# Attention scores on 32 rows per head, with zero matmuls in place of repeated score matmuls

## The chip, the cores and the metric

The kernel runs on one core of a Trainium2 chip. The metric is device time of one launch in microseconds (us), median over the runs. Engines are called by their names in the profile: PE multiplies matrices, PEld loads its stationary operand, ACT applies functions element by element, DVE does vector work, POOL a few small things and some of the transfers, SP issues most transfers.

## What is computed

Two layers, each an attention block A and a token-mixing block B, both with a residual. Sequence S = 2048, width D = 640, 32 heads of 20 columns, F = 1536, inputs in bf16.

```python
def _A_ref(x, wqkv, wo):
    qkv = (x @ wqkv).reshape(B, S, 3, H, Dh) ...
    q, k, v = qkv[0], qkv[1], qkv[2]
    scores = jnp.einsum("bhqd,bhkd->bhqk", q, k) * (Dh ** -0.5)
    p = _softmax(scores, axis=-1)
    o = jnp.einsum("bhqk,bhkd->bhqd", p, v)
    return o ... @ wo

def _B_ref(x, w1, b1, w2, b2):
    h = _layernorm(x, axis=-1)
    u = gelu(jnp.einsum("bsd,sf->bdf", h, w1) + b1)
    return (jnp.einsum("bdf,fs->bds", u, w2) + b2) transposed

x = x + _A_ref(_layernorm(x), A_wqkv, A_wo)
x = x + _B_ref(_layernorm(x), ...)
x = x + _A_ref(_layernorm(x), A_wqkv, A_wo)
x = x + _B_ref(_layernorm(x), ...)
```

Each layer has 32 x 2048 x 2048 scores, 134 million, and every one goes through an exponential on ACT.

## The kernel before

**Stages.** A first stage normalizes x and forms the values V and the first head group's keys and queries. Then follow, for each layer, `attention`, `mixer_mm1` and `mixer_mm2`; the mixer of layer 0 also prepares the attention of layer 1. The change lies in `attention`, which runs twice.

**Layout.** Heads go in 8 groups of 4. A group's transposed keys `KT` and queries `QTq` have 128 partitions: each head's 20 rows stand at the start of a block of 32, and the other 12 rows are zero. `Vaug` holds 20 value columns, a column of ones (which yields the softmax denominator) and padding to 32 columns for each head.

**Units and tiles.** A unit is one block of 512 queries (`qb`, 4 of them), one head group `g` (8) and one block of 128 keys (`kt`, 16), 512 units in all. A unit has four chunks, one per head, each of 128 keys x 512 queries. `HORDER` gives the heads' order in a unit. Three chunks in a row, across unit borders, make one PSUM tile `S` of 128 x 1536; there are 683 a layer (the last has two chunks). `S` has two buffers (6 PSUM banks), the output accumulator `acc` one bank, the tile `misc` for all other products one bank.

**Scores** (`s_matmul`, L320). The stationary operand is `KT` on 64 rows, that is two heads' keys at once. So that only one head's score comes out, the moving operand is a copy of the queries in which every second head's rows are multiplied by zero: `prep_block` makes `qev` and `qod` on DVE (L279, L280), once for each of the 32 pairs of query block and group in a layer. Heads 0 and 2, or 1 and 3, lie on different halves of the rows, and `HORDER` (0, 2, 1, 3) puts such a pair side by side.

**The repeat** (`emit_S`). If no other product is planned for the tile, the tile's three score matmuls are issued twice (`R_DEFAULT=1`); the second pass writes the same values again, and the exponential waits for the last of them.

**Exponential** (`emit_exp`, L348): one ACT instruction a tile, 128 x 1536 from PSUM to a bf16 tile `P` (5 buffers).

**Outputs** (`emit_PV`, L546): four matmuls a unit, each with 128 rows and 32 columns of `Vaug`, into the four 32-partition quarters of `acc`. After the last key block `normalize` reads `acc` on DVE (L357 to L364), and the next group takes the one `acc` buffer.

**Order.** PE executes in the order the program is written, held by a chain over all its instructions. For each tile t the loop emits the scores of tile t+1, the exponential of t, the outputs whose exponentials are complete up to tile t-1 (none or one unit), and then some fills. Fills are the other products of the stage: key and query projections (L227), the output projection (L448, L481), the first part of the token-mixing product (L421). `emit_fills` takes 1.5 units of cost if the tile has outputs and 3 if not, and pauses one tile after each finished group; `planned_fill` says beforehand whether there will be any.

The scores of tile t+1 wait for the exponential of t-1, because it reads the same `S` buffer. The scheduling loop:

```python
for t in range(NTILES):
    has_fill = planned_fill()
    reps = 0 if has_fill else CFG["R_DEFAULT"]
    if t + 1 < NTILES:
        emit_S(t + 1, reps)
    emit_exp(t)
    ...
    emit_fills(CFG["FILL_PV"] if n_pv else CFG["FILL_NOPV"], misc_alloc)
```

Of the kernel before, what the change touches and what calls it, by code (L numbers as in the profile page):

```python
# [11 lines left out]
BF16 = mybir.dt.bfloat16  # L12
F32 = mybir.dt.float32
ACT = mybir.ActivationFunctionType
ALU = mybir.AluOpType
# [9 lines left out]
VW = 24  # L25

CFG = dict(
    R_DEFAULT=1,
    FILL_NOPV=3.0,
    FILL_PV=1.5,  # L30
    PV_LAGT=1,
# [8 lines left out]
def kernel(  # L40
# [12 lines left out]
    nc = tc.nc  # L53
# [4 lines left out]
    NKT = NT  # L58
# [6 lines left out]
    def pe(inst):  # L65
        tc.chain_iter_dep("pe_order", inst.ins)
        return inst
# [12 lines left out]
    consts = ctx.enter_context(tc.tile_pool(name="consts", bufs=1))  # L80
# [6 lines left out]

    ident = consts.tile([128, 128], BF16, name="ident")
    make_identity(nc, ident[:])
    mask_ev = consts.tile([128, 1], F32, name="mask_ev")  # L90
    mask_od = consts.tile([128, 1], F32, name="mask_od")
    for blk in range(4):
        nc.vector.memset(mask_ev[32 * blk:32 * blk + 32, :], 1.0 if blk % 2 == 0 else 0.0)
        nc.vector.memset(mask_od[32 * blk:32 * blk + 32, :], 0.0 if blk % 2 == 0 else 1.0)
    mhalf = consts.tile([128, 1], F32, name="mhalf")
    nc.vector.memset(mhalf[:], -0.5)
    warm = consts.tile([128, 1], F32, name="warm")
    nc.gpsimd.tensor_tensor(out=warm[:], in0=mhalf[:], in1=mhalf[:], op=ALU.mult)
    nc.gpsimd.tensor_tensor(out=warm[:], in0=warm[:], in1=mhalf[:], op=ALU.pow)
    x1lp = ctx.enter_context(tc.tile_pool(name="x1lp", bufs=1))  # L100
    x1last = x1lp.tile([128, 4, D], F32, name="x1last")
    hhp = ctx.enter_context(tc.tile_pool(name="hhp", bufs=1))
# [92 lines left out]
    def get_QT(st, qb):  # L195
        if qb not in st.QTq:
            st.QTq[qb] = st.qtp.tile([128, NG, 512], BF16, name="QTq")
        return st.QTq[qb]
# [45 lines left out]
    def attention(st, x_in_ap, x_mid, uacc_l):  # L244
        layer = st.layer
        KT, hT = st.KT, st.hT
        with ExitStack() as p1:
# [7 lines left out]
            ustg = p1.enter_context(tc.tile_pool(name=f"ustg{layer}", bufs=2))  # L255
            h2_tiles = {}
            ptp = p1.enter_context(tc.tile_pool(name=f"ptp{layer}", bufs=CFG["PT_BUFS"]))
            qmp = p1.enter_context(tc.tile_pool(name=f"qmp{layer}", bufs=2))
            atp = p1.enter_context(tc.tile_pool(name=f"atp{layer}", bufs=2))
            x1acc = {}  # L260
            LASTQB = NQB - 1
# [1 line left out]

            units = [(qb, g, kt) for qb in range(NQB) for g in range(NG) for kt in range(NKT)]
            NU = len(units)
            S_tiles, P_tiles, acc_tiles, qm_tiles, attnT_tiles = {}, {}, {}, {}, {}
            fill_queue = deque()
            fill_state = dict(cur=None, idx=0, tile=None, cooldown=0, unit=0)
            proj_enqueue_done = [False]
            in_attention = [True]  # L270
            tt_state = {}

            def prep_block(qb, g):
                if (qb, g) in qm_tiles:
                    return
                qe = qmp.tile([128, 512], BF16, name="qev")
                qo = qmp.tile([128, 512], BF16, name="qod")
                src = get_QT(st, qb)[:, g, :]
                nc.vector.tensor_scalar(out=qe[:], in0=src, scalar1=mask_ev[:, 0:1], scalar2=None, op0=ALU.mult)  # L279
                nc.vector.tensor_scalar(out=qo[:], in0=src, scalar1=mask_od[:, 0:1], scalar2=None, op0=ALU.mult)  # L280
                qm_tiles[(qb, g)] = (qe, qo)

            HORDER = (0, 2, 1, 3)
            chunks = [(n, j) for n in range(NU) for j in HORDER]
            NCH = len(chunks)
            NTILES = (NCH + 2) // 3

            def on_unit_start(n):
                qb_n, g_n, kt_n = units[n]
                fill_state["unit"] = n  # L290
                if qb_n == 0 and kt_n == 0:
                    if g_n + KQA < NG:
                        enqueue_kq_for_group(g_n + KQA)
                    if g_n == max(0, NG - KQA) and NQB > 1:
                        enqueue_qproj(1)
                if qb_n >= 1 and g_n == 0 and kt_n == 2 and qb_n + 1 < NQB:
                    enqueue_qproj(qb_n + 1)
                if not proj_enqueue_done[0]:
                    last_k_block = max(0, NG - 1 - KQA)
                    if NQB == 1:  # L300
                        done = (qb_n == 0 and g_n >= last_k_block)
                    elif NQB == 2:
                        done = (qb_n == 0 and g_n >= max(0, NG - KQA)) or qb_n >= 1
                    else:
                        done = (qb_n == NQB - 2 and (g_n > 0 or kt_n >= 2)) or qb_n > NQB - 2
                    proj_enqueue_done[0] = done
                check_hT_dead()
                if kt_n == 0:
                    ensure_ready(qb_n, g_n)
                    prep_block(qb_n, g_n)  # L310
                if kt_n == NKT // 2 and n + NKT < NU:
                    nqb, ng, _ = units[n + NKT - kt_n]
                    if ("Q", nqb, ng) not in pending_keys():
                        prep_block(nqb, ng)

            def s_matmul(St, slot, n, j):
                qb, g, kt = units[n]
                jj = j // 2
                q = qm_tiles[(qb, g)][j % 2]
                pe(nc.tensor.matmul(St[:, slot, :], lhsT=KT[64 * jj:64 * jj + 64, g, kt * 128:(kt + 1) * 128],  # L320
                                    rhs=q[64 * jj:64 * jj + 64, :], start=True, stop=True,
                                    tile_position=(64 * jj, 0)))

            def emit_S(t, reps):
                cs = chunks[3 * t:3 * t + 3]
                for (n, j) in cs:
                    if j == HORDER[0]:
                        on_unit_start(n)
                St = sps.tile([128, 3, 512], F32, name="S")
                S_tiles[t] = St  # L330
                for _rep in range(reps + 1):
                    i = 0
                    while i < len(cs):
                        n, j = cs[i]
                        if i + 1 < len(cs) and cs[i + 1][0] == n and (j, cs[i + 1][1]) in ((0, 2), (1, 3)):
                            s_matmul(St, i, n, j)
                            s_matmul(St, i + 1, n, cs[i + 1][1])
                            i += 2
                        else:
                            s_matmul(St, i, n, j)  # L340
                            i += 1

            def emit_exp(t):
                St = S_tiles.pop(t)
# [176 lines left out]
            def pending_keys():  # L521
                keys = set()
                if fill_state["cur"] is not None:
                    keys.add(fill_state["cur"]["key"])
                for grp in fill_queue:
                    keys.add(grp["key"])
                return keys
# [9 lines left out]
            def emit_PV(n):  # L537
# [23 lines left out]
            def emit_fills(budget, pool_alloc):  # L561
                fs = fill_state
                if fs["cooldown"] > 0:
                    fs["cooldown"] -= 1
                    return 0.0
                spent = 0.0
                while spent < budget:
                    if fs["cur"] is None:
                        if not fill_queue:
                            break  # L570
                        if fill_queue[0].get("not_before", 0) > fs["unit"] and budget < 100:
                            break
# [12 lines left out]
                return spent  # L585
# [10 lines left out]

            LAGT = CFG["PV_LAGT"]
            pv_done = 0
            emit_S(0, 0)
            for t in range(NTILES):  # L600
                has_fill = planned_fill()
                reps = 0 if has_fill else CFG["R_DEFAULT"]
                if t + 1 < NTILES:
                    emit_S(t + 1, reps)
                emit_exp(t)
                n_pv = 0
                while pv_done < NU and (4 * pv_done + 3) // 3 <= t - LAGT:
                    emit_PV(pv_done)
                    pv_done += 1
                    n_pv += 1  # L610
                emit_fills(CFG["FILL_PV"] if n_pv else CFG["FILL_NOPV"], misc_alloc)
            in_attention[0] = False
            while pv_done < NU:
# [245 lines left out]
```

## Time and profile before

| | |
|---|---|
| time, median of 3 runs | 2105.06 us (2104.55 to 2106.12) |
| the profiled execution: time, span | 2106.7 us, 2104.9 us |
| exponentials of layer 0, first start to last end | 49.79 to 972.49 us |
| exponentials of layer 1, first start to last end | 1093.53 to 2017.59 us |
| PE matmuls in the span | 13278 |
| of them scores (L320), outputs (L546) | 6014, 4096 |
| mean granted clock of PE | 0.992 |

The span runs from the first to the last instruction. "Busy" of PE counts a matmul up to its modelled end, 0.376 to 0.39 us for 512 columns, while the next one of the same kind starts 0.2155 us later; so a PE that is busy all the time need not be full. The granted clock is 1.00 or 0.50 in any one moment. It was 0.50 from the start to 18.2 us (as far as the records reach), from 973.9 to 991.0, from 1086.6 to 1090.0, from 2021.8 to 2035.5 us and at the very end, and 1.00 in all other places. Its changes all lie on one grid of 3.413 us.

### The profile page before, as it was taken

Reading aid. Unit: us, or ns where it says so; the run is one execution under the profiler, and the core shown is the slowest. Engines: PE = TensorE matmul, PEld = TensorE weight load, DVE = VectorE, ACT = ScalarE, POOL = GpSimd, SP = SyncE. Lnnn points to the kernel's source line nnn. Section 1 sums busy time; section 2 is a strip of 40 time slices with the busy share of each in tenths; the row PEclk is TensorE's granted clock in tenths of the full one; section 3 lists DMA queues with packets and bytes.
Section 4 is the critical chain, followed back from the end, with each engine's and each line's share of the span. In section 5 each row is a group of like instructions: output and inputs, shape, how many; then the busy total and the mean of one; then the engine's idle time right before and its main releaser. Section 6 shows DMA issues by size and latency. Waiting matters only on the chain.

```text
span 2104.9 us, 31825 instructions
## 1 busy us (share of the span) xinstructions
PE 1953.5 (93%) x13278; PEld 657.3 (31%) x13278; DVE 570.0 (27%) x1231; ACT 1931.5 (92%) x1504; POOL 148.2 (7%) x218
## 2 busy tenths in 40 slices
PE   7999999999999999997999999999999999999979
PEld 4222222233223332223542222222332233222335
DVE  6122222221322132223642122322113220322242
ACT  5999999999999999996349999999999999999952
POOL 2000000110012001110000000001100120011000
PEclk9999999999999999998999999999999999999989
DMA  5000000110034012223620000001101340222245
GB/s 129 1 1 1 1 18 22 61 53 10 29 58 71 1 35 44 37 26 118 211 81 1 1 1 1 26 28 65 47 14 38 66 63 1 57 49 36 38 121 182
DMA packets 90737, 96.88 MB, mean 46 GB/s; under 512 B 9696, under 2 KB 68192, under 8 KB 90592
## 3 DMA queue, kind: packets, MB, share of 16 engines
q1 hardware_dynamic: 70464, 71.22, 11.0%
q0 software_dynamic: 20128, 23.62, 7.5%
q8 instruction: 104, 1.70, 0.3%
q14 instruction: 41, 0.34, 0.1%
HBM read 55.48 MB, written 39.32 MB: 45 GB/s over the span
## 4 chain that ended last, share of the span: by engine, by line
ACT 58%; PE 25%; issue 13%; DVE 3%; DMA 1%; POOL 0%; SPq 0%; DVEq 0%; ACTq 0%; POOLq 0%
ACT P L348 58%; PE S L320 10%; PE y L741 4%; PE acc L546 3%; PE misc L227 3%; PE pp L218 2%; PE big L670 1%; PE misc L448 1%; DMA ua<-uacc 1%; PE pp L227 0%; DVE T L357 0%; PE S L481 0%; DMA x0in<-in_A_x_dram 0%; DVE bnst L158 0%; PE misc L481 0%
## 5 line engine op out<-in xcount | busy, mean ns | idle before, releaser
L348 ACT ACTIVATE P<-S 128x1536 bf16<-128x1536 f32 (+1 forms) x1366 | 1839.9, 1500 | 8.3 <-PE S L320 7.0
L320 PE MATMUL S<-qev,KT 64*128 64x512 bf16 x2962 | 836.8, 377 | 96.2 <-ACT P L348 90.1
L320 PE MATMUL S<-qod,KT 64*128 64x512 bf16 x3052 | 838.2, 379 | 9.1 <-ACT P L348 4.6
L320 PEld LDWEIGHTS <-KT 64*128 64x128 bf16 x6014 | 326.7, 93 | 655.5 <-issue 486.4
L546 PE MATMUL acc<-P,Vaug 128*32 128x512 bf16 x4096 | 409.9, 389 | 6.2 <-DVE T L357 4.3
L546 PEld LDWEIGHTS <-Vaug 128*32 128x32 bf16 x4096 | 106.5, 92 | 439.0 <-issue 439.0
L427 DVE COPY ustg<-misc 128x512 f32<-128x512 f32 (+1 forms) x144 | 70.0, 486 | 296.6 <-PE misc L421 296.5
L169 POOL TENSOR_TENSOR rstd<-veps,mhalf 128x1 f32<-128x1 f32 x64 | 35.5, 554 | 1187.6 <-DVE veps L164 1068.4
L432 POOL DMA_DIRECT2D uacc<-ustg x96 | 83.0, 864 | 473.6 <-DVE ustg L427 444.3
L421 PE MATMUL misc<-h2st,w1st 128*128 128x512 bf16 (+1 forms) x576 | 115.8, 303 | 0.0
L741 PE MATMUL y<-uT,w2s 128*128 128x512 bf16 (+1 forms) x768 | 107.8, 299 | 3.4 <-ACT uT L684 3.4
L508 DVE CAST QTq<-misc 128x512 bf16<-128x512 f32 x62 | 42.8, 691 | 214.2 <-PE misc L227 214.2
L227 PE MATMUL misc<-hh,wq_pad 128*128 128x512 bf16 x310 | 98.9, 385 | 0.0
L357 DVE STREAM_TRANSPOSE T<-acc 128x512 f32<-128x512 f32 x64 | 45.9, 717 | 186.4 <-PE acc L546 186.4
L508 DVE CAST KT<-misc 128x512 bf16<-128x512 f32 x56 | 38.7, 691 | 212.9 <-PE misc L227 212.9
L227 PE MATMUL misc<-hh,wk_pad 128*128 128x512 bf16 x280 | 87.2, 385 | 0.0
L279 DVE TENSOR_SCALAR qev<-QTq,mask_ev 128x512 bf16<-128x512 bf16 x64 | 22.6, 353 | 235.4 <-PE S L320 234.8
L448 PE MATMUL misc<-wo_pad,attnT 128*128 128x512 bf16 (+1 forms) x384 | 76.8, 303 | 0.0
L741 PEld LDWEIGHTS <-w2s 128*128 128x128 bf16 x768 | 59.6, 98 | 49.9 <-issue 5.0
L76 ACT CAST Vaug<-pp 128x500 bf16<-128x500 f32 (+1 forms) x32 | 14.3, 453 | 52.5 <-PE pp L218 52.5
L457 DVE TENSOR_TENSOR x1s<-misc,xin 128x512 f32<-128x512 f32 (+1 forms) x48 | 23.5, 489 | 131.5 <-PE misc L448 131.5
L218 PE MATMUL pp<-wv,hh 128*128 128x500 bf16 (+1 forms) x320 | 52.0, 313 | 1.7 <-DVE hh L78 1.5
(77 smaller groups left out, 715.9 us busy)
## 6 DMA issues: line engine op xcount, KB each, us to landing
uacc<-ustg POOLq DMA_DIRECT2D x72, 256.0 KB, 4.0
w2s<-in_B_w_dram SPq DMA_DIRECT2D x16, 768.0 KB
w1st<-in_B_w_dram SPq DMA_DIRECT2D x36, 256.0 KB
xd<-x1s SPq DMA_DIRECT2D x24, 320.0 KB
x1in<-xd SPq DMA_DIRECT2D x24, 320.0 KB
ua<-uacc SPq DMA_DIRECT2D x24, 320.0 KB
xd<-x2s SPq DMA_DIRECT2D x16, 320.0 KB
xin<-xd SPq DMA_DIRECT2D x16, 320.0 KB
```

The lines of the kernel that those rows point to most:

```text
L218: pe(nc.tensor.matmul(pp[:, 0:c1 - c0], lhsT=st.hT[:, dt_, tt * 128:(tt + 1) * 128], rhs=wv[:, dt_, c0:c1], start=(dt_ == 0), stop=(dt_ == ...
L227: pe(nc.tensor.matmul(t[:, :], lhsT=wpad[:, dt_, g, :], rhs=st.hT[:, dt_, tb * 512:(tb + 1) * 512], start=(dt_ == 0), stop=(dt_ == NDT - 1)))
L320: pe(nc.tensor.matmul(St[:, slot, :], lhsT=KT[64 * jj:64 * jj + 64, g, kt * 128:(kt + 1) * 128], rhs=q[64 * jj:64 * jj + 64, :], start=Tru ...
L348: nc.scalar.activation(out=P[:, 0:ncs, :].rearrange("p a b -> p (a b)"), in_=St[:, 0:ncs, :].rearrange("p a b -> p (a b)"), func=ACT.Exp, ...
L357: nc.vector.transpose(out=T1[:], in_=acc[:])
L421: pe(nc.tensor.matmul(t[:, 0:w], lhsT=states[fp]["w"][:, sti, ftl * 128:(ftl + 1) * 128], rhs=tiles4[sti][:, c0:c1], start=(sti == 0), sto ...
L427: nc.vector.tensor_copy(out=stg[:, 0:w], in_=t[:, 0:w])
L432: nc.gpsimd.dma_start(out=dst, in_=stg[:, 0:w], accum_op=ALU.add)
L448: pe(nc.tensor.matmul(t[:, 0:w], lhsT=attnT[:, g, ttl * 128:(ttl + 1) * 128], rhs=wo_pad[:, g, c0:c1], start=(g == 0), stop=(g == NG - 1)))
L508: nc.vector.tensor_copy(out=dst_ap, in_=t[:, :])
L546: pe(nc.tensor.matmul(acc[32 * j:32 * j + 32, :], lhsT=Vaug[:, (kt * H + hh) * VW:(kt * H + hh) * VW + 32], rhs=P[:, ci % 3, :], start=(kt ...
L741: pe(nc.tensor.matmul(y[:, 0:w], lhsT=w2s[:, ft, sl * 128:(sl + 1) * 128], rhs=uT[:, ft, c0:c1], start=(ft == 0), stop=(ft == NF - 1)))
```

## The change

- The scores are computed head by head: the stationary operand is one head's 32 rows of `KT`, the moving operand the same 32 rows of the unmasked queries `QTq`. `HORDER` becomes (0, 1, 2, 3), so that any three chunks in a row lie on three different blocks of 32 rows. The tiles keep their 1536 columns.
- The masks, `qev`, `qod` and `prep_block` go.
- The second pass over the scores goes. Instead `keep_busy` issues matmuls of a zero stationary operand `zw` (128 x 32) with a moving operand of ones `zr` (128 x 512), four at a time, that add zeros to the four quarters of the open `acc`. They come after a tile's outputs, and only if no fill is planned: three rounds of four if the tile has no outputs, two rounds if it has (`SLOTS` less one for the scores and one for each unit of outputs). Where no `acc` is open, between a group's last outputs and the next group's first, none are issued.
- POOL sets `zw` and `zr` once at the start.

In the built program PE has 16569 matmuls in place of 13278: 4096 score matmuls in place of 6014, 5208 zero matmuls, all others as before. In 600 of the 1366 turns of the loop there are zero matmuls (1302 rounds of four). ACT's instructions and their order are the same. On DVE the 128 mask multiplications and the 8 mask settings are gone. On SP the first three loads of `x1in` for the last mixer, which stood ahead of the loads of `w2s`, stand behind the first four loads of `ua`; on POOL the two bias loads stand a few places later.

```diff
 CFG = dict(
-    R_DEFAULT=1,
+    SLOTS=4,
...
-    mask_ev = consts.tile([128, 1], F32, name="mask_ev")
-    mask_od = consts.tile([128, 1], F32, name="mask_od")
-    for blk in range(4):
-        nc.vector.memset(mask_ev[32 * blk:32 * blk + 32, :], 1.0 if blk % 2 == 0 else 0.0)
-        nc.vector.memset(mask_od[32 * blk:32 * blk + 32, :], 0.0 if blk % 2 == 0 else 1.0)
...
+    zw = consts.tile([128, 32], BF16, name="zw")
+    nc.gpsimd.memset(zw[:], 0.0)
+    zr = consts.tile([128, 512], BF16, name="zr")
+    nc.gpsimd.memset(zr[:], 1.0)
...
-            def prep_block(qb, g):
...
-            HORDER = (0, 2, 1, 3)
+            HORDER = (0, 1, 2, 3)
...
             def s_matmul(St, slot, n, j):
                 qb, g, kt = units[n]
-                jj = j // 2
-                q = qm_tiles[(qb, g)][j % 2]
-                pe(nc.tensor.matmul(St[:, slot, :], lhsT=KT[64 * jj:64 * jj + 64, g, kt * 128:(kt + 1) * 128],
-                                    rhs=q[64 * jj:64 * jj + 64, :], start=True, stop=True,
-                                    tile_position=(64 * jj, 0)))
-
-            def emit_S(t, reps):
+                pe(nc.tensor.matmul(St[:, slot, :], lhsT=KT[32 * j:32 * j + 32, g, kt * 128:(kt + 1) * 128],
+                                    rhs=get_QT(st, qb)[32 * j:32 * j + 32, g, :], start=True, stop=True,
+                                    tile_position=(32 * j, 0)))
+
+            def emit_S(t):
...
-                for _rep in range(reps + 1):
-                    i = 0
-                    while i < len(cs):
...
+                for i, (n, j) in enumerate(cs):
+                    s_matmul(St, i, n, j)
+
+            def keep_busy(count):
+                for acc in acc_tiles.values():
+                    for _ in range(count):
+                        for j in range(4):
+                            pe(nc.tensor.matmul(acc[32 * j:32 * j + 32, :], lhsT=zw[:], rhs=zr[:], start=False,
+                                                stop=False, skip_group_check=True, tile_position=(0, 32 * j)))
...
             for t in range(NTILES):
                 has_fill = planned_fill()
-                reps = 0 if has_fill else CFG["R_DEFAULT"]
                 if t + 1 < NTILES:
-                    emit_S(t + 1, reps)
+                    emit_S(t + 1)
                 emit_exp(t)
...
+                if not has_fill:
+                    keep_busy(CFG["SLOTS"] - 1 - n_pv)
                 emit_fills(CFG["FILL_PV"] if n_pv else CFG["FILL_NOPV"], misc_alloc)
```

More of the change, by code (lines that the diff above doesn't have):

```diff
@@ L257, in attention @@
             ptp = p1.enter_context(tc.tile_pool(name=f"ptp{layer}", bufs=CFG["PT_BUFS"]))
-            qmp = p1.enter_context(tc.tile_pool(name=f"qmp{layer}", bufs=2))
             atp = p1.enter_context(tc.tile_pool(name=f"atp{layer}", bufs=2))
@@ L265, in attention @@
             NU = len(units)
-            S_tiles, P_tiles, acc_tiles, qm_tiles, attnT_tiles = {}, {}, {}, {}, {}
+            S_tiles, P_tiles, acc_tiles, attnT_tiles = {}, {}, {}, {}
             fill_queue = deque()
@@ L271, in attention @@
             tt_state = {}
-            def prep_block(qb, g):
[L274 to L281, printed above, removed]
-            HORDER = (0, 2, 1, 3)
+            HORDER = (0, 1, 2, 3)
             chunks = [(n, j) for n in range(NU) for j in HORDER]
@@ L309, in on_unit_start @@
                     ensure_ready(qb_n, g_n)
[L310 to L314, printed above, removed]
             def s_matmul(St, slot, n, j):
                 qb, g, kt = units[n]
-                jj = j // 2
-                q = qm_tiles[(qb, g)][j % 2]
-                pe(nc.tensor.matmul(St[:, slot, :], lhsT=KT[64 * jj:64 * jj + 64, g, kt * 128:(kt + 1) * 128],
-                                    rhs=q[64 * jj:64 * jj + 64, :], start=True, stop=True,
-                                    tile_position=(64 * jj, 0)))
-            def emit_S(t, reps):
+                pe(nc.tensor.matmul(St[:, slot, :], lhsT=KT[32 * j:32 * j + 32, g, kt * 128:(kt + 1) * 128],
+                                    rhs=get_QT(st, qb)[32 * j:32 * j + 32, g, :], start=True, stop=True,
+                                    tile_position=(32 * j, 0)))
+            def emit_S(t):
                 cs = chunks[3 * t:3 * t + 3]
@@ L330, in emit_S @@
                 S_tiles[t] = St
-                for _rep in range(reps + 1):
-                    i = 0
-                    while i < len(cs):
[L334 to L341, printed above, removed]
+                for i, (n, j) in enumerate(cs):
[6 more added lines that the diff above has]
+                                                stop=False, skip_group_check=True, tile_position=(0, 32 * j)))
             def emit_exp(t):
@@ L598, in attention @@
             pv_done = 0
-            emit_S(0, 0)
+            emit_S(0)
             for t in range(NTILES):
                 has_fill = planned_fill()
-                reps = 0 if has_fill else CFG["R_DEFAULT"]
                 if t + 1 < NTILES:
-                    emit_S(t + 1, reps)
+                    emit_S(t + 1)
                 emit_exp(t)
```

## Prediction

> **What bounds the kernel now.** I read the page first: busy times, clock row, chain, groups. Then the waits, the instructions in order of time around one late exponential and one ordinary stretch, and the clock in single stretches of 3.41 us.
>
> ```profile
> PE 1953.5 (93%) x13278; PEld 657.3 (31%) x13278; DVE 570.0 (27%) x1231; ACT 1931.5 (92%) x1504; POOL 148.2 (7%) x218
> ...
> L348 ACT ACTIVATE P<-S 128x1536 bf16<-128x1536 f32 (+1 forms) x1366 | 1839.9, 1500 | 8.3 <-PE S L320 7.0
> ```
>
> PE and ACT both look full. But ACT is busy without a gap in both attentions: 8.3 us of idle time ahead of 1366 exponentials. The timeline, ordinary stretch:
>
> ```profile
> 401.91 0.54 PEld L320 LDWEIGHTS <-KT 64*128 64x128 bf16 x6 [0.42 <-issue]
> ...
> 402.88 0.40 PE L546 MATMUL acc<-P,Vaug 128*32 128x512 bf16 x4
> ...
> 403.21 0.39 PE L320 MATMUL S<-qod,KT 64*128 64x512 bf16 x2
> 403.44 0.38 PE L320 MATMUL S<-qev,KT 64*128 64x512 bf16 x1
> 403.74 0.23 PEld L421 LDWEIGHTS <-w1st 128*128 128x128 bf16 x4 [0.42 <-issue]
> ```
>
> A score tile computed twice takes PE 0.97 us (401.91 to 402.88), outputs 0.33, scores computed once 0.53. Single starts in the trace give the parts: a pair of 64-row scores starts 0.003 us apart, the next 512-column matmul of the same kind 0.2155 later (one slot), and a change of kind costs 0.09 on top (score to outputs 0.304). Three scores in two 64-row halves are thus two slots, the repeat makes four. The starts of exponentials step by 1.343 us in the median. A repeated tile with outputs fills five slots and two changes, 1.26 us of 1.343: little slack. Where that goes wrong:
>
> ```profile
> 79.17 0.82 PE L227 MATMUL misc<-hh,wk_pad 128*128 128x512 bf16 x3
> 79.92 0.54 PEld L320 LDWEIGHTS <-KT 64*128 64x128 bf16 x6 [0.42 <-issue]
> ...
> 80.58 0.38 PE L320 MATMUL S<-qod,KT 64*128 64x512 bf16 x1
> ...
> 81.05 1.45 ACT L348 ACTIVATE P<-S 128x1536 bf16<-128x1536 f32 x1 [0.26 <-PE S L320]
> ```
>
> Three fills, then a repeated score tile: its last, useless matmul starts at 80.58 and the exponential 0.473 later, after 0.26 idle; the usual overlap of two exponentials (0.17) is lost in part too, so this one ends 0.37 late. I went through all starts of L348. 65 exponentials start 0.472 or 0.473 us after their last score matmul, the smallest distance that occurs, and lose 10.3 us in sum against the 1.343 step (5.1 in layer 0, 5.3 in layer 1). Ten others lose 2.2 us with the scores long done (0.75 us before); the eight in layer 1 lie 86 to 87 us, 64 exponentials, or twice that apart. They are ACT's own. So PE costs the attentions 10.3 us, and 1.343 x 1364 = 1832 us of the span is ACT at its own pace, which this change does not touch.
>
> The clock, stretches on its grid (columns: stretch, length, busy time of PE, PEld, DVE, ACT, POOL, granted clock, DMA share, GB/s):
>
> ```profile
> 970.51:973.92 3.41, 1.82 (x13) 0.39 (x9) 0.90 (x2) 1.98 (x2) 0.00 (x0) 1.00 0.00 0
> 973.92:977.33 3.41, 1.24 (x5) 0.53 (x6) 2.64 (x6) 0.00 (x0) 0.00 (x0) 0.50 0.86 287
> 1083.15:1086.56 3.41, 1.32 (x19) 0.98 (x17) 2.84 (x9) 0.28 (x1) 0.55 (x1) 1.00 0.77 235
> 1086.56:1089.97 3.41, 3.41 (x15) 1.60 (x13) 0.80 (x2) 0.58 (x1) 0.00 (x0) 0.50 0.65 207
> 1902.35:1905.76 3.41, 2.73 (x21) 0.86 (x20) 1.90 (x5) 3.41 (x4) 0.86 (x1) 1.00 0.51 69
> 2014.99:2018.40 3.41, 2.43 (x18) 0.66 (x17) 0.33 (x1) 2.60 (x3) 0.00 (x0) 1.00 0.32 78
> 2018.40:2021.81 3.41, 0.53 (x4) 0.29 (x5) 2.82 (x6) 0.00 (x0) 0.00 (x0) 1.00 1.14 308
> ```
>
> A stretch with PE busy 1.82, 1.32 or 0.53 of 3.41 us is followed by one at half clock; one with 2.43 or more is not. A full stretch at half clock (1086.56) brings the clock back. So the repeat is also what keeps PE warm, and its replacement has to.
>
> **The change, part by part.**
>
> *Repeat out, 32-row scores in.* 1918 score matmuls go. Three scores on three row blocks have no row of their own; nearest is the pair on two halves, 0.003 us apart, so I take one slot, 0.22 us. The other end is no overlap, 0.65. With one slot the last score starts some 0.06 us after the exponential that frees its buffer, and its own exponential could start 0.53 after that, where ACT is ready only at 1.343 - 0.17 = 1.17. PE may be 0.64 us late in a tile before ACT notices. In the example above the scores would start at 79.92 as now and be good for an exponential at 80.40; ACT is ready at 80.68. All 65 late starts have a repeat or two slots between the fills and the exponential, and go: -10.3 us. The ten of ACT stay.
>
> *First tile.* The first exponential of a layer waits for the second slot (scores at 49.11 and 49.33, exponential 49.79): one slot less, 0.21 us, twice: -0.4.
>
> *Zero matmuls.* 1302 rounds of four. Row for one: four outputs, which start within 0.012 us; a round behind a round of the same kind is a slot of 0.2155, or at most the 0.32 seen from outputs to a fill, with a change between. A tile with zero matmuls is then four slots and two changes, 1.04 us (1.26 at the dear end), of 1.343: hidden behind the exponential; with that cover gone each round would cost its 0.22, 280 us in all. What is queued behind them is the next scores, and these wait for ACT until 1.343 anyway. They wait for nothing new: they write the open `acc`, after its first outputs have waited for DVE. A fill tile needs 4 slots and three changes, 1.13 us.
>
> *Rate of issue.* Such a tile sends 15 pairs of load and matmul in 1.343 us, 90 ns each. The trace has 29 pairs in 2.69 us (93 ns, at 1013 us), 85 in 10 us (118 ns). At 90 or less it costs nothing. At 118 the tile takes 1.77 us; tiles with zero matmuls mostly alternate with fill tiles of 8 pairs, whose mean fits, but nine runs of 18 to 20 in a row, some 175 tiles, would lose 0.43 each: 75 us. At 93: 9 us. I take 0, for the dense row ends where work, not issue, changes.
>
> The Trainium skill ("TensorE: Matmul & The Clock Gate", Back-to-back issue gap) puts a sustained stream of load and matmul at about 81 ns a pair for 128 columns, which would be 1.22 us for such a tile, inside 1.343; no run here shows it.
>
> *Clock.* A full tile keeps PE busy from the score's start to 0.17 after the last slot, 1.13 us of 1.343, so 2.87 in 3.41: above 2.43. Between two groups no `acc` is open. There a tile has scores and outputs (busy 0.70), and, where the next unit's fourth chunk falls one tile later, the one after has scores alone (0.39). In the built order 14 such places in both layers have no fill. A stretch of 2.54 tiles that holds both is busy 0.70 + 0.39 + 0.54 x 1.13 = 1.70, under 1.82. About one position of the grid in five holds both, another quarter falls between 1.82 and 2.43: 3 to 6 lost stretches. One at half clock does 3.41 / 2.0 = 1.7 tiles of four slots in place of 2.54, 1.1 us, of which some 0.5 is covered by the 0.64 above: 0.6 us. I take four: +2.5 us; bounds 0 and 14 x 1.1 = 15.
>
> The skill (same page, What's actually happening) says that the clock falls after at least one idle window of about 3.4 us. The trace is stricter: the stretch at 970.51 had PE busy 53% and was followed by half clock. By the page this term would be 0 and the sum 2.5 us lower.
>
> *The rest.* `qev` and `qod` (0.35 us each on DVE, 27% busy) lie beside ACT; the first pair at 39 us, in a stage where DVE works 0.7 of the time, may give up to 0.7 us; I take 0. POOL's two settings go into its idle time before 7 us. `x1in` behind `ua`: 0.98 MB more between 2020 and 2037, where the queue is empty from 2029 to 2037 and `x1in` is first read at 2051: 0. The half-clock stretches after each attention start on the grid, wherever the attention ends; either may come out a part of a stretch longer or shorter: 0, bounds -3 and +3.
>
> **Sum:** -10.3 - 0.4 + 2.5 = -8.2 us. The profiled execution took 2106.7 (span 2104.9), 1.6 above the median; against the median 2105.06 - 8.2 = 2097 us.
>
> **Rivals.**
>
> *The clock eats it.* If the limit is nearer 2.43, all 14 places and some with one thin tile lose a stretch: +8 to +15, in sum 2102 to 2109. For: nothing is seen between 1.82 and 2.43. Against: few grid positions hold both thin tiles.
>
> *The clock does not count zero matmuls* (slower). The place is the tile with zero matmuls, real work there 0.70 of 1.343, 1.78 in 3.41, under 1.82. Then the 175 tiles in long runs run cold at 2.0 us, +0.65 each, 114 us: about 2210; if the alternating ones follow (600 tiles, 390 us), 2485. It decides as soon as adding zeros counts as less than about half a matmul. For: the trace has no matmul on constants. Against: nothing in the trace ties the clock to values; PE issues them like outputs.
>
> *Three row blocks do not overlap* (the change does not do what it says). A tile has six slots and two changes, 1.47 us: +0.13 on 600 to 1366 tiles, 2173 to 2270. Against: two halves overlap to 0.003 us.
>
> *Issue is the bound.* 2097 + 9 to 75, so 2106 to 2172.
>
> **Chances.** Forecast 65% (its own range 2092 to 2103), clock eats it 14%, zeros not counted 9%, no overlap 5%, issue 7%. A difference of 0.2%, 4.2 us, is about what can be told. Faster takes the forecast, 65%; same is 2100.9 to 2109.3, the clock rival and the cheap end of issue, 16%; slower the rest, 19%. The range goes from 2091 to 2118, which leaves out the dear rivals.
>
> **What would show it.** Right: exponentials step by 1.343 with only ACT's own ten late ones; L320's three scores within 0.01 us; PE's busy share near 80% in the attentions, clock 1.00 but for single stretches at group borders. Wrong: idle time ahead of L348 put down to scores, long stretches at 0.50 where zero matmuls stand (zeros not counted), scores 0.2 apart, or pairs more than 90 ns apart with the clock at 1.00.

## The result and the profile after

| | before | after |
|---|---|---|
| median | 2105.33 us | 2101.18 us |
| 14 runs each | 2103.76 to 2107.29 | 2096.18 to 2104.62 |
| profiled execution: time, span | 2106.7, 2104.9 | 2096.18, 2094.4 |
| mean granted clock, profiled | 0.992 | 0.985 |

The ratio is 0.9977, with a 95% interval of 0.9969 to 0.9985: 4.1 us less, half of the 8.2 forecast. The runs now spread over 8.4 us, before over 3.5, and the profiled execution after is the shortest of its 14. So its trace shows 10.5 us of gain, of which 5.0 are its distance from the median after and 1.4 the distance of the profiled execution before from its own.

The page after, its busy times and then its groups (busy time, mean ns of one, idle time ahead of it):

```profile
PE 1739.4 (83%) x16568; PEld 658.0 (31%) x16568; DVE 528.0 (25%) x1095; ACT 1927.4 (92%) x1504; POOL 148.2 (7%) x220
...
L327 ACT ACTIVATE P<-S 128x1536 bf16<-128x1536 f32 (+1 forms) x1366 | 1835.9, 1888 | 5.5 <-PE S L301 5.3
L301 PE MATMUL S<-QTq,KT 32*128 32x512 bf16 x4096 | 541.0, 383 | 314.0 <-ACT P L327 284.8
...
L525 PE MATMUL acc<-P,Vaug 128*32 128x512 bf16 x4096 | 414.1, 393 | 0.8 <-DVE T L336 0.5
L319 PE MATMUL acc<-zr,zw 128*32 128x512 bf16 x5208 | 390.5, 383 | 0.0
```

Scores now wait longer for ACT (284.8 us of their idle time, 94.7 before). What idle time is left ahead of the exponentials is 5.5 us, and 5.3 of it still waits for scores. I went through the starts: none of these is a late tile of the old kind. 1.07 us stand ahead of the first exponentials of the two layers (0.536 each, before 0.725); the other 4.4 lie in eleven stretches at half clock inside the attentions, or up to 3 us behind them. Before there was no such stretch in the attentions. Here is the one after 738 us, by stretches of the clock's grid (columns as in the prediction: stretch, length, busy PE, PEld, DVE, ACT, POOL, clock, DMA share, GB/s), with three others that lost the clock and one that kept it:

```profile
335.23:338.65 3.42, 2.09 (x20) 0.80 (x18) 1.60 (x3) 3.42 (x4) 0.00 (x0) 1.00 0.02 5
594.65:598.06 3.41, 2.16 (x20) 0.78 (x17) 2.09 (x4) 3.41 (x4) 0.00 (x0) 1.00 0.80 287
738.01:741.42 3.41, 1.65 (x21) 0.57 (x13) 2.03 (x4) 3.41 (x4) 0.00 (x0) 1.00 0.00 0
741.42:744.83 3.41, 3.41 (x30) 0.71 (x27) 0.34 (x1) 3.41 (x3) 0.00 (x0) 0.50 0.02 5
912.09:915.50 3.41, 1.84 (x21) 0.69 (x24) 3.01 (x5) 3.41 (x4) 0.86 (x1) 1.00 0.35 32
1577.69:1581.10 3.41, 2.33 (x24) 1.04 (x21) 2.75 (x5) 3.41 (x4) 0.00 (x0) 1.00 0.00 0
```

After 335.23, 594.65, 738.01 and 912.09 the next stretch is at half clock; after 1577.69 it is not. One stretch at half clock, in which PE has no gap (741.42), brings the clock back. The instructions in order of time around 738 (start, length, engine, what, idle time before):

```profile
738.51 0.39 PE L301 MATMUL S<-QTq,KT 32*128 32x512 bf16 x3 [0.19 <-ACT P L327]
...
738.84 0.40 PE L525 MATMUL acc<-P,Vaug 128*32 128x512 bf16 x4
...
739.86 0.39 PE L301 MATMUL S<-QTq,KT 32*128 32x512 bf16 x3 [0.62 <-ACT P L327]
...
741.20 0.44 PE L301 MATMUL S<-QTq,KT 32*128 32x512 bf16 x3 [0.95 <-ACT P L327]
...
741.57 0.62 PE L525 MATMUL acc<-P,Vaug 128*32 128x512 bf16 x4
...
741.97 1.07 PE L319 MATMUL acc<-zr,zw 128*32 128x512 bf16 x8
...
745.94 2.92 ACT L327 ACTIVATE P<-S 128x1536 bf16<-128x1536 f32 x2 [0.77 <-PE S L301]
```

This is a border between two groups: a tile of scores and outputs (738.51), a tile of scores alone (739.86), no zero matmuls, because no `acc` is open. Two tiles later each instruction takes longer (outputs 0.62 in place of 0.40), and ACT stands still for 0.77 us at 745.94. All eleven begin within three key blocks after such a border.

Where the time went in the two profiled executions, by stage:

| stage | before | after | change |
|---|---|---|---|
| to the first exponential | 49.79 | 49.30 | -0.5 |
| attention of layer 0 | 922.71 | 920.95 | -1.8 |
| between the attentions | 121.04 | 119.56 | -1.5 |
| attention of layer 1 | 924.06 | 919.33 | -4.7 |
| to the end | 87.35 | 85.27 | -2.1 |

Counted against the step of 1.343 us, the exponentials lost 12.9 us before and 6.4 after; this is the 6.5 of the two attentions. So the late exponentials of before are gone (10.3 forecast, and the 2.2 put down to ACT), and the eleven stretches gave back 5.9, 0.54 each: this is what the exponentials in them or just behind them end late, and no other ends more than 0.03 us late. The rest, 0.3 to 0.5, is there before and after. Over all 14 runs the mean clock stands for 18.4 to 27.1 half-clock stretches in the span ((1 - clock) x 2 x span / 3.413), 22.8 in the mean; 7 of the profiled 18 lie outside the attentions. The median run thus has some 14 to 15 inside, an estimate, and time rises with their number by 0.875 us each (a line through the 14 runs, correlation 0.93). That is more than the 0.54 in the trace; why is open.

### The profile page after: what moved, and what is told of

It is laid out like the page before. It is cut to its first block, busy times and chain, and to the rows that moved or that the text cites. A ratio compares the mean times of both kernels' runs of the same rounds, so it can differ in the third digit from the quotient of the medians.

```text
span 2094.4 us, 38271 instructions
## 1 busy us (share of the span) xinstructions
PE 1739.4 (83%) x16568; PEld 658.0 (31%) x16568; DVE 528.0 (25%) x1095; ACT 1927.4 (92%) x1504; POOL 148.2 (7%) x220
## 4 chain that ended last, share of the span: by engine, by line
ACT 68%; issue 17%; PE 12%; DVE 2%; DMA 1%; POOL 0%; SPq 0%; DVEq 0%; ACTq 0%; POOLq 0%
ACT P L327 67%; PE y L721 5%; PE S L301 1%; PE pp L217 1%; PE acc L525 1%; PE big L650 1%; PE misc L226 1%; DMA ua<-uacc 1%; PE misc L400 1%; PE acc L319 0%; PE pp L226 0%; PE S L460 0%; DMA x0in<-in_A_x_dram 0%; DVE bnst L157 0%; DVE x1last L473 0%
## 5 line engine op out<-in xcount | busy, mean ns | idle before, releaser
L327 ACT ACTIVATE P<-S 128x1536 bf16<-128x1536 f32 (+1 forms) x1366 | 1835.9, 1888 | 5.5 <-PE S L301 5.3
L301 PE MATMUL S<-QTq,KT 32*128 32x512 bf16 x4096 | 541.0, 383 | 314.0 <-ACT P L327 284.8
L301 PEld LDWEIGHTS <-KT 32*128 32x128 bf16 x4096 | 243.5, 91 | 796.5 <-issue 759.6
L525 PE MATMUL acc<-P,Vaug 128*32 128x512 bf16 x4096 | 414.1, 393 | 0.8 <-DVE T L336 0.5
L319 PE MATMUL acc<-zr,zw 128*32 128x512 bf16 x5208 | 390.5, 383 | 0.0
L319 PEld LDWEIGHTS <-zw 128*32 128x32 bf16 x5208 | 129.6, 96 | 90.9 <-issue 26.5
```

Of the source, the lines that this page charges most:

```text
L301: pe(nc.tensor.matmul(St[:, slot, :], lhsT=KT[32 * j:32 * j + 32, g, kt * 128:(kt + 1) * 128], rhs=get_QT(st, qb)[32 * j:32 * j + 32, g, : ...
L319: pe(nc.tensor.matmul(acc[32 * j:32 * j + 32, :], lhsT=zw[:], rhs=zr[:], start=False, stop=False, skip_group_check=True, tile_position=(0, ...
L327: nc.scalar.activation(out=P[:, 0:ncs, :].rearrange("p a b -> p (a b)"), in_=St[:, 0:ncs, :].rearrange("p a b -> p (a b)"), func=ACT.Exp, ...
L525: pe(nc.tensor.matmul(acc[32 * j:32 * j + 32, :], lhsT=Vaug[:, (kt * H + hh) * VW:(kt * H + hh) * VW + 32], rhs=P[:, ci % 3, :], start=(kt ...
```

## The experiments

My theory after the result: the borders without zero matmuls cost the clock, and the clock costs the missing half of the gain. Rivals: the 32-row scores or the rate of issue cost it, or zeros count for less than data does. Ratios are against the kernel before on the same chip.

**Zeros at the borders.** Where no `acc` is open, the zeros go into a `misc` tile that nobody reads.

```diff
-                for acc in acc_tiles.values():
+                targets = list(acc_tiles.values())
+                open_acc = bool(targets)
+                if not open_acc and count > 0:
...
+                    targets = [miscp.tile([128, 512], F32, name="misc")]
+                for acc in targets:
...
-                            pe(nc.tensor.matmul(..., start=False,
+                            pe(nc.tensor.matmul(..., start=not open_acc,
```

> The change, plus zero matmuls into the free PSUM tile misc where no acc is open (between a group's last outputs and the next group's first), so that every turn without a fill has four slots. Theory (clock lost at group borders): no stretch at half clock inside either attention, next to no idle time ahead of the exponentials, median 2092 to 2096 us, and the spread of the runs falls from 8 us to 3 or less. Rival (the remaining loss and the spread come from between the stages): 2099 to 2103 us and a spread of about 8 us as with the change.

Measured: 2093.1 us (2090.21 to 2095.04, 5 runs), ratio 0.9934 (0.9921 to 0.9948). The theory holds in the main: 13 us under the kernel before, and the attentions' loss is 1.6 us. The spread stays wider than expected, 4.8 us, and not all stretches are gone. The exponentials' group, a stretch that lost the clock, and PE in it:

```profile
L332 ACT ACTIVATE P<-S 128x1536 bf16<-128x1536 f32 (+1 forms) x1366 | 1834.7, 1972 | 1.9 <-PE S L301 1.9
```

```profile
316.88:320.29 3.41, 2.31 (x29) 1.15 (x29) 0.94 (x3) 3.41 (x4) 0.00 (x0) 1.00 0.00 0
```

```profile
317.89 0.45 PE L432 MATMUL misc<-wo_pad,attnT 128*128 128x128 bf16 x5
318.58 0.39 PE L301 MATMUL S<-QTq,KT 32*128 32x512 bf16 x3 [0.23 <-ACT P L332]
318.91 0.34 PE L432 MATMUL misc<-wo_pad,attnT 128*128 128x128 bf16 x3
319.92 0.39 PE L301 MATMUL S<-QTq,KT 32*128 32x512 bf16 x3 [0.68 <-ACT P L332]
```

Three stretches are still lost in the profiled execution, all where the tile's fills are 128-column pieces of the output projection: five of them take 0.45 us, two of 512 columns 0.60. The planner counts them as a filled tile.

**Five slots in place of four**, borders as in the change.

```diff
-    SLOTS=4,
+    SLOTS=5,
```

> The change with five slots in place of four (one more round of four zero matmuls wherever there are any; none at the borders, as before). Theory: the tiles beside a border are fuller, a border stretch rises from 1.70 to about 1.82 busy of 3.41 us, so about half of the 11 lost stretches go: 2096 to 2100 us. Rival (the clock needs a higher mean, not the border): nearly all lost stretches go, 2092 to 2095. Rival (PE gets too full, 1.26 us of 1.343): late exponentials come back, 2103 or more.

Measured: 2100.45 us (2097.78 to 2102.87, 5 runs), ratio 0.9972 (0.996 to 0.9984). The profiled execution has eleven stretches at half clock, in eight places, but it is one of the two coldest of its five (clock 0.985; all five 0.984 to 0.989). Counted by the clock as above, with the 8 that lie outside the attentions here, the median run has some 7 inside, an estimate: half of the 14 to 15 did go, as expected. The time did not follow to 2096 to 2100, as a cold stretch costs 0.8 us here (8.9 lost in the profiled execution) in place of 0.54. Five slots at half clock fit a tile still less than four, which may be why; one place stayed cold for three stretches.

**No zeros at all.**

```diff
-    SLOTS=4,
+    SLOTS=1,
```

> The change without any zero matmuls. Theory (they hold the clock): tiles without fills have PE busy 0.70 of 1.343 us at most, the clock falls in most of the attention, over 100 stretches at half clock, and fill tiles (four slots, 2.0 us cold) make the exponentials late: 2130 us or more. Rival (zeros count little for the clock): about as the change, some 10 to 20 lost stretches and 2097 to 2105 us.

Measured, one run: 2173.29 us, mean clock 0.763, 290 half-clock stretches in the attentions. The clock row, in tenths of full speed, and the exponentials:

```profile
PEclk9877788875887576575998898888668775766669
...
L327 ACT ACTIVATE P<-S 128x1536 bf16<-128x1536 f32 (+1 forms) x1366 | 1855.8, 1534 | 57.3 <-PE S L301 46.0
```

Zeros do hold the clock, and are worth some 70 us.

**Zeros on data.** The moving operand of the zero matmuls is a piece of `KT` in place of ones.

```diff
-    ... lhsT=zw[:], rhs=zr[:], ...
+    ... lhsT=zw[:], rhs=KT[:, 0, 512 * (j % NQB):512 * (j % NQB) + 512], ...
```

> The change with key data as the moving operand of the zero matmuls in place of ones (the stationary operand stays zero, so acc does not change). Theory (the clock counts instructions, not values): 7 to 20 lost stretches in the attentions and 2096 to 2105 us, as with the change. Rival (constant data count less): 0 to 3 lost stretches, 2092 to 2095 us.

Measured, one run: 2099.9 us, clock 0.983, twelve stretches at half clock in the attentions. The values make no difference that one run can show.

**The scores of before, once, with zeros.** The 64-row masked scores stay; only their repeat is replaced, by the zero matmuls of the change with one round less, as two slots go to the scores.

```diff
-    R_DEFAULT=1,
+    SLOTS=4,
...
-                reps = 0 if has_fill else CFG["R_DEFAULT"]
+                reps = 0
...
+                if not has_fill:
+                    keep_busy(CFG["SLOTS"] - 2 - n_pv)
```

> The kernel before (64-row scores from masked queries) without the repeat, with zero matmuls that fill four slots: scores two slots, one or two rounds of zeros. It has the change's zeros without its 32-row scores. Theory (the gain comes from taking the repeat away; the 32 rows only spare PE a slot): the late exponentials of the repeat go, the borders are less thin (scores two slots), so fewer stretches are lost than the change's 11: 2094 to 2100 us. Rival (the 32 rows are what makes the exponentials punctual): late exponentials remain, 2102 us or more.

Measured: 2093.79 us (2093.47 to 2096.6, 5 runs), ratio 0.9945 (0.9933 to 0.9957); one stretch lost in the profiled execution.

```profile
L359 ACT ACTIVATE P<-S 128x1536 bf16<-128x1536 f32 (+1 forms) x1366 | 1834.9, 1772 | 1.7 <-PE S L324 1.4
```

So taking the repeat out from between scores and exponential is enough for the gain. The 32-row scores add nothing to it; at the borders, where nothing stands in for the slot they save, they cost some 7 us (0.9945 against 0.9977).

**The 32-row scores three times, no zeros.**

```diff
+                for _rep in range(reps + 1):
+                    for i, (n, j) in enumerate(cs):
+                        s_matmul(St, i, n, j)
...
+                    emit_S(t + 1, 0 if has_fill else 2)
...
-                if not has_fill:
-                    keep_busy(CFG["SLOTS"] - 1 - n_pv)
```

> The change's 32-row scores, but with the scores computed three times where no fill is planned, in place of the zero matmuls (three slots with or without an open acc). Theory: the last pass is done 0.49 us after the freed buffer, so exponentials are late only after long fill tiles, 1 to 4 us in sum; the borders keep three or four slots and only tiles with narrow fills lose the clock, 0 to 5 stretches: 2093 to 2098 us. Rival (repeats cost as much as in the kernel before): 2102 us or more.

Measured: 2100.19 us (2095.37 to 2107.21, 12 runs), ratio 0.9974 (0.9963 to 0.9984), against 2093 to 2098 expected. Its profiled execution, the shortest, lost six stretches, two of them with PE streaming 48% of the time, more than many that keep the clock elsewhere; the last run below bears on that. By the clock of all twelve (0.977 to 0.988) the median run lost some ten, an estimate, in place of 0 to 5. The repeat itself no longer costs anything: outside the half-clock stretches and the 3 us behind them no exponential ends late in this profile, where 75 did before (12.5 us in all). This fits a repeat that was dear by its length: four slots with two passes before, three with three passes here.

**Zeros where fills are narrow too.** The first experiment, and zeros behind fills that leave slots empty.

```diff
...
+                    slots += 1.0 if grp["cost"][fs["idx"]] == 1.0 else 0.26
...
+                if has_fill and acc_tiles:
+                    keep_busy(int(CFG["SLOTS"] - 1 - n_pv - used + 0.5))
```

> The bridged version, plus zero matmuls after the fills of a tile when these fill too few slots (the 128-column fills of the output projection, which stood in the last three stretches before the clock fell). Theory: no stretch at half clock inside the attentions, exponentials wait under 1 us in sum, median 2090 to 2093. Rival (these three were chance, or the added rounds make scores late): 2093 to 2096 and some lost stretches.

Measured: 2093.47 us (2092.57 to 2096.19, 5 runs), ratio 0.9944 (0.9932 to 0.9956). The profiled execution lost one stretch in place of three, but the one before was the coldest of its five, and the clocks of the two versions overlap (0.990 to 0.994 and 0.991 to 0.993). There is no gain in the median either: what is left there is below what these runs can tell.

**Zeros in the stages after the attentions too.**

```diff
+            def warm(rounds):
+                w = miscp.tile([128, 512], F32, name="misc")
...
+            warm(10)
...
+                warm(2)
+            warm(16)
```

> The version before it, plus zero matmuls into misc after each attention's last outputs and between and after the tail's projections, where PE waits for DVE and the clock fell for 4 to 5 stretches in every run so far. Theory (the clock costs there too): at most one stretch lost at each end of attention, the tail projections and the first matmuls of the mixer (L670 of the kernel before) run at full clock, 3 to 5 us less at each end: 2082 to 2088 us. Rival (the ends are bound by DVE and the loads, or the zeros delay the projections): 2089 us or more.

Measured: 2095.23 us (2094.18 to 2097.64, 5 runs), ratio 0.995 (0.9937 to 0.9963): no half clock in the attentions or behind them but for two single stretches between the two, clock 0.998, and no time won. The chain that ended last, first of the version with warm stages, then of the one before it (start, length, what):

```profile
2018.08 3.64 PE misc L610 x64
2021.71 9.90 PE big L669 x72
...
2032.55 2.87 DMA ua<-uacc
...
2039.80 49.29 PE y L740 x361
```

```profile
2018.39 4.99 PE big L659 x24
...
2025.04 3.98 DMA ua<-uacc
...
2037.77 49.29 PE y L730 x361
```

From the last exponential (2007.75 and 2005.72) to the last product's start is 32.05 us in both: the warm rounds take 3.64 us of the chain themselves, and then it waits for a load. As far as this chain shows, the cold clock after the attentions is hidden anyway.

**What the clock counts.** With ten profiles I could ask which stretches lose the clock. I counted the stretches at full clock that lie wholly between the first and the last exponential of a layer. By streaming time alone (512 columns are taken as 0.2133 us at full clock, half of the 0.427 between starts of 512-column matmuls at half clock) stretches with up to 48% lost it, and others kept it from 35% on; weighted with rows x columns of the array in use, none of 4814 over 40% lost it. So: the changed kernel with the same rounds of zeros on a quarter of the array, 128 rows by 32 columns, and on half.

```diff
-                        for j in range(4):
+                        for j in range(1):
```

> The zero matmuls keep their number of rounds and their slots, but each round is one matmul into one quarter of the accumulator in place of four into all four: PE streams for the same time on a quarter of its rows x columns. If the clock goes by the time in which PE streams at all (4 slots x 0.2133 of 1.343 us = 0.64 in a tile with zeros, as in the changed kernel), it stays at 0.985 +- 0.01 with 8 to 20 lost stretches in the attentions and the time at 2096 to 2105 us. If it goes by streaming weighted with rows x columns in use (scores 0.75 of the array, outputs 1, zeros 0.25: on average 2.06 slots x 0.2133 / 1.343 = 0.33, under the 0.36 to 0.40 where the ten profiles so far divide), long runs of such tiles go cold: 100 stretches or more, clock 0.80 to 0.93, time 2110 to 2170 us.

> As the one-quarter version, with two of the four quarters in each round. By streaming time alone: clock 0.985 +- 0.01. Weighted with rows x columns: 0.75 + 0.75 + 2.25 x 0.5 = 2.63 slots, 0.42 of the time, just over the division at 0.36 to 0.40: 15 to 60 lost stretches, more than the changed kernel's 11, clock 0.95 to 0.985, 2097 to 2115 us.

Measured, one run each: 2100.17 us, clock 0.982, 13 stretches at half clock in the attentions, and 2097.84 us, 0.985, 10. The theory of the area fell; the columns make no difference that can be seen. In all profiles so far it was only the scores that used less than all rows, so the weight could still be the rows. The transpose, 32 rows by 128 columns:

```diff
-    zw = consts.tile([128, 32], BF16, name="zw")
+    zw = consts.tile([128, 128], BF16, name="zw")
...
-                        for j in range(4):
-                            pe(nc.tensor.matmul(acc[32 * j:32 * j + 32, :], lhsT=zw[:], rhs=zr[:], ...
-                                                tile_position=(0, 32 * j)))
+                        pe(nc.tensor.matmul(acc[:], lhsT=zw[0:32, :], rhs=zr[0:32, :], ..., tile_position=(0, 0)))
```

> The zero matmuls keep their rounds and slots; each round is one matmul on 32 rows and all 128 columns, which adds zeros to the whole accumulator. It is the transpose of the one-quarter version (128 rows, 32 columns), which kept the clock at 0.982. If streaming time alone counts, the same comes out: clock 0.975 to 0.99, 8 to 20 lost stretches in the attentions, 2096 to 2105 us. If streaming time weighted with the share of the 128 rows counts, which divides the stretches of the twelve profiles so far a little better than streaming time alone (45 against 54 of 6015 on the wrong side of one limit, 0.37 against 0.415), such tiles have 0.75 + 0.75 + 2.25 x 0.25 = 2.06 slots, 0.33 of the time: 100 stretches or more go cold, clock 0.80 to 0.93, 2110 to 2170 us.

Measured, one run: 2309.6 us, clock 0.781, 283 stretches at half clock in the attentions. It is dearer than expected: the exponentials end late by 0.75 us for each of them, without any zeros by 0.27, so tiles with zeros fit a cold stretch worse. The clock rows and the zero matmuls of the two, 128 rows by 32 columns first:

```profile
PEclk9999999999999999998999999999999999999989
...
L319 PE MATMUL acc<-zr,zw 128*32 128x512 bf16 x1302 | 387.2, 386 | 0.0
```

```profile
PEclk9988987866987585665998786898668965777659
...
L318 PE MATMUL acc<-zr,zw 32*128 32x512 bf16 x1302 | 530.0, 506 | 0.0
```

Here a stretch with PE busy 2.61 of 3.41 us is followed by half clock:

```profile
71.87:75.28 3.41, 2.61 (x22) 0.93 (x20) 0.69 (x1) 3.41 (x4) 0.00 (x0) 1.00 0.00 0
```

Apart from the width of `zw` the two kernels differ only in the form of 1302 matmuls, with the same slots. All full-clock stretches in the attentions of the 13 profiles, counted as above, by the time in which PE streams, each moment weighted with the share of the 128 rows in use:

```
share of 3.41 us    stretches   next one at half clock
under 0.32                50     49
0.32 to 0.36             105     96
0.36 to 0.40             197     70
over 0.40               6065      0
```

By streaming time without the weight, 10 of 4760 stretches over 0.56 lose the clock, and the best single limit puts 105 on the wrong side in place of 57. The threefold scores fit this: if each of their slots counts three quarters, a border tile of nine score matmuls has 3 x 0.75 x 0.2133 / 1.343 = 0.36, and five of the six lost stretches also hold 128-column fills. But that three scores side by side count three quarters is fitted, not shown by a run of its own: counted as full, with the 32-row zeros still at a quarter, the best limit puts 68 on the wrong side. All 32-row zeros also lie on the same row block; other blocks were not tried.

## Why the prediction came out as it did

- **The late exponentials** went as forecast, all 65, for the reason given. **The first tile** too: the idle time ahead of the first exponential of a layer fell by 0.19 us, twice.
- **"The ten of ACT stay"** was wrong: their 2.2 us went too. They were not ACT's own. The exponential's instruction now begins earlier and lies over its predecessor longer (mean duration 1888 ns against 1500 at the same step of 1.343), but by which path this removes the ten was not tried and stays open.
- **Zero matmuls hidden**: yes. Their group has 0.0 us of idle time ahead, and a tile with them fits. "A fill tile needs 4 slots" holds for 512 columns and fails for the 128-column ones.
- **Three row blocks overlap**: the three scores start within 0.010 us of each other. That rival is gone.
- **Rate of issue, 0 us**: right. After, 237 pairs go in 20 us (84 ns a pair), and the version with warm stages has 52 pairs in 2.69 us (52 ns). The Trainium skill ("TensorE: Matmul & The Clock Gate", Back-to-back issue gap) gives 81 ns as sustained for 128 columns and 131 ns for 512, and the 237 pairs are all of 512 columns: its figure for these matmuls was not the one that the prediction took, and the measurement, which decides, lies under 131.
- **The clock, +2.5 us**: this is the term that failed, in its count. The price of a lost stretch was about right (0.6 forecast, 0.54 in the trace), the places too. But "I take four" should have been eleven in the profiled execution (+5.9 us) and some 14 in the median one (+7.6). I had set the limit by PE's busy time, between 1.82 and 2.43 us, counted with the lower end, and took every tile with a fill as full. That nothing was seen in between was a slip: outside the attentions the trace of before has stretches with 2.21 (at 1004.64) and 2.35 us (at 2049.11), and both kept the clock. In the changed kernel stretches with 1.65 to 2.17 lost it. Busy time is also not what decides: 2.31 lost it in the experiment with bridged borders, 2.33 kept it here, 2.61 lost it with 32-row zeros. With the row weight the thin tiles are thinner than I made them: a tile of scores alone counts 0.16 of its 1.343 us, where I put 0.39 of busy time. The same page (What's actually happening) puts the fall to half clock after an idle window; no lost stretch inside the attentions was idle (PE was busy 1.65 us or more in each), and this rule would have forecast none of the eleven. The two stretches of before, each with the next one:

```profile
1004.64:1008.05 3.41, 2.21 (x19) 1.33 (x19) 2.08 (x5) 2.47 (x4) 0.00 (x0) 1.00 0.21 26
1008.05:1011.47 3.42, 3.12 (x28) 1.85 (x27) 2.55 (x9) 0.92 (x1) 0.55 (x1) 1.00 0.97 358
2049.11:2052.53 3.42, 2.35 (x19) 1.31 (x19) 1.85 (x3) 1.80 (x4) 0.00 (x0) 1.00 0.00 0
2052.53:2055.94 3.41, 3.41 (x26) 1.88 (x25) 1.02 (x2) 0.88 (x2) 0.00 (x0) 1.00 0.51 144
```

- **"The clock eats it"**, the rival at 2102 to 2109, was thus nearer in the number of lost stretches; the result lies just under it, because the ten of ACT paid 2.2 us that neither had counted. That these two misses have opposite signs, and that the forecast so came out nearer than its clock term, is luck.
- **"The clock does not count zero matmuls"** is false for this form and would have been true for another: with zeros on 32 rows the kernel takes 2309.6 us. The forecast had no ground to know which.
- **The ends**: -1.5 and -2.1 us in the profiled execution. The stretch between the attentions went from 119.25 to 121.72 us over the three versions with bridged borders, filled narrow tiles or 64-row scores, whose work there is the same, the tail from 85.95 to 86.73: the bounds of 3 were about right, and nothing there belongs to the change.

The sum with the measured terms: -10.3 - 2.2 - 0.4 + 14 x 0.54 = -5.3; measured -4.1. With the 0.875 us from the line through the runs it would be -0.7; the price of a stretch in the median run lies in between and is not settled.

## What to carry to other kernels

Work that only keeps an engine awake belongs behind what others wait for, or must be short enough in front of it; taking it from there was worth 12 to 13 us here, and the change gave most of that back where its filler had nowhere to write. When filler or real work is made leaner, look for the places with no filler, and count activity as the clock did in these profiles, in streaming weighted with the rows in use, not in busy time. The versions with bridged borders (2093.1), with 64-row scores and zeros (2093.79) and with filled narrow tiles (2093.47) lie 0.55 to 0.66% under the kernel before and 0.3 to 0.4% under the changed one, and the runs do not tell them apart.

## What the hardware showed that I had not expected

- The clock of PE falls for the next 3.41 us if, in one stretch of its grid, streaming weighted with the rows in use is under about 0.36 (145 of 155), and never did over 0.40 (6065 stretches). Columns and values made no difference that could be seen: one matmul of 128 rows by 32 columns of zeros held the clock as well as four (0.982 and 0.985, one run with one), one of 32 rows by 128 columns did not (0.781, one run).
- Three matmuls on different row blocks share one slot, with starts within 0.010 us; that together they count only three quarters for the clock is the better fit (57 against 68 stretches on the wrong side), not shown by itself.
- Pairs of weight load and matmul can follow each other every 52 ns over 2.69 us (128 rows by 32 columns, 512 moving columns, in the version with warm stages).
